# Linear attention and a two-layer MLP on one core: q of the first 512 tokens in runs of four, shared output banks, and a written order up to layer 1

## The chip, the core and the metric

The kernel runs on one core of one Trainium2 chip. Its time is the device time of one execution in microseconds, the median of the runs. A core has TensorE (PE; weight loads are listed as PEld), VectorE (DVE), ScalarE (ACT), GpSimd (POOL) and SyncE (SP), each with a queue that runs in order, and 16 DMA engines that all queues share. SP issues the loads of q, k and v; POOL issues the weights, which are cast from float32 to bfloat16 on the way, and most of the output.

## What is computed

Causal linear attention with a decay per head, in blocks with a running state, for 4 sequences of 768 tokens, 8 heads of 64; then a two-layer MLP (512 to 2048 to 512) on the 3072 tokens. `lam` lies between 0.97 and 0.99.

```python
for b in range(nb):
    qb, kb, vb = q[:, :, sl], k[:, :, sl], v[:, :, sl]
    intra = np.einsum('bhic,bhjc->bhij', qb, kb) * Dmask        # lam**(i-j) for i >= j
    intra = np.einsum('bhij,bhjd->bhid', intra, vb)
    inter = np.einsum('bhid,bhde->bhie', qb * lam_pow, kv_state)
    out[:, :, sl] = intra + inter
    kv_state = lam_block * kv_state + np.einsum('bhsd,bhse->bhde', kb * rev_pow, vb)
x = out.transpose(0, 2, 1, 3).reshape(B * S, H * D)
h = x @ w_in
g = np.where(h >= 1, h, np.where(h <= -1, 0.0, (h + 1) ** 2 / 4))
return g @ w_out
```

## The kernel before

**The first 512 tokens.** They are worked in four units: unit u = 2*sc + r has the 256 tokens of half sc (0 or 1) and the four heads of group r. For each unit SP loads q, k and v (`e_load`, 256 KB each). Partition p holds tokens 2p and 2p+1 of the half for four heads, so each run in memory is two tokens of one head, 512 B. `e_cast` multiplies q and k by a table of powers of `lam` and writes bfloat16 (k on DVE, q on POOL), and casts v. `e_t` transposes q or k on TensorE (four 128 by 128 transposes), `e_tc` copies the result to SBUF. `e_upd` adds k times v to the running state in PSUM, `e_st` copies the state to SBUF. `e_s` forms the scores into two PSUM banks of the pool `pp_s` (one for each parity of the head), `e_m` multiplies them by the causal mask on DVE. `e_sp` multiplies the state by q and starts the output in two fresh banks of `pp_y`; `e_o` adds the masked scores times v. `e_x` copies the output as bfloat16 into `xT`, the input of layer 1, whose first 512 columns therefore hold even tokens ahead of odd ones within each 128.

**Then.** The rest of the tokens comes in chunks of 128 (`f_load`, `cast`, and so on, from chunk 4). Layer 1 (`f_l1`, 8 matmuls of 256 columns a group for the first 512 tokens) goes to a bank of `pp_h` or `pp_y`; `f_r` on ACT and `f_g` on DVE apply the activation; `f_l2` is layer 2; `f_y` copies, `f_out` writes. For the first 512 tokens `f_out` issues two DMAs for each 128 rows, one for even and one for odd tokens. The weights come in nine slices (`f_w`, `WSL`): two of `w_in` of 256 columns, three of 512, four of `w_out`. Slice 0 is issued once k of unit 2 has landed (`GATE_W`); the first load of chunk 4 waits for slice 7 (`GL`).

**What sets the order.** Nearly every step is an entry made by `add(key, engine, ns, function, needs, due=...)`. `run_plan` simulates the engines with these costs, picks on each engine the ready entry with the earliest due time, and emits the steps in that order; matmuls on zeros (`warm`) fill TensorE's gaps before layer 1. Two waits outside the plan matter: `e_o` of units 0 and 1 waits for a state copy, and that of units 2 and 3 drains TensorE first. The needs of the plan that the change touches:

```python
add(("s", "e", u), "PE", 250, lambda u=u: e_s(u),
    [("kT", "e", u), ("qT", "e", u), ("m", "e", u - 1, 1)], ...)
add(("sp", "e", u), "PE", 300, lambda u=u: e_sp(u),
    [("st", "e", u, 1), ("st", "e", u, 0), ("x", "e", u - 1, 0), ("x", "e", u - 1, 1), ("qT", "e", u)], ...)
```

So the scores of a unit wait for both masks of the unit before, and the output of a unit waits until the one before has been copied out.

Of the kernel before, what the change touches and what calls it, by code (L numbers as in the profile page):

```python
# [8 lines left out]
F32 = mybir.dt.float32  # L9
BF16 = mybir.dt.bfloat16  # L10
# [13 lines left out]
def kernel(  # L24
# [73 lines left out]
    pos_ei = const.tile([128, 2, 2], I32)  # L98
    nc.gpsimd.iota(pos_ei, pattern=[[2 * C, 2], [1, 2]], base=-S // 2, channel_multiplier=2)
# [4 lines left out]
    pos_e = const.tile([128, NE], F32)  # L104
# [28 lines left out]
    def tables(pos, n, name):  # L133
        arg = const.tile([128, n, H], F32, name="arg" + name)
        nc.vector.tensor_tensor(arg, _bc(pos, 2, H), _bc(ln_lam, 1, n), op=AX.mult)
        tk = const.tile([128, n, H], F32, name="tk" + name)
        nc.scalar.activation(out=tk, in_=arg, func=AF.Exp, scale=-1.0)
        tq = const.tile([128, n, H], F32, name="tq" + name)
        nc.scalar.activation(out=tq, in_=arg, func=AF.Exp)
        return tq, tk  # L140

    tab_e = tables(pos_e, NE, "e")
    mask2 = const.tile([128, 2, 2, 64], F32)
    mask2b = const.tile([128, 2, 2, 64], F32)
    for t, base in ((mask2, 0), (mask2b, 128)):
        nc.gpsimd.memset(t, 1.0)
        nc.gpsimd.affine_select(
            out=t, in_=t, compare_op=AX.is_ge, fill=0.0,
            base=base, pattern=[[-1, 2], [1, 2], [2, 64]], channel_multiplier=-2)
# [11 lines left out]
    tab = tables(pos, NCB, "d")  # L161
# [21 lines left out]
    ops, OPS = [], {}  # L183
# [12 lines left out]
    def run_plan(free):  # L196

        users = {x.key: [] for x in ops}
        for x in ops:
            x.needs = [OPS[y] for y in x.keys if y in OPS]  # L200
            for y in x.needs:
                users[y.key].append(x)
# [100 lines left out]
    def get_xT(s):  # L303
        if s not in xT:
            xT[s] = xp.tile([128, KO, MS], BF16, name="xT", tag="xT")
        return xT[s]
# [6 lines left out]
    def e_load(u, x):  # L313
        sc, r = divmod(u, 2)
        t = ld.tile([128, HR, 2 * D], F32, name=f"x{x}f", tag=f"x{x}f")
        s0 = sc * 2 * C
        ld_dma["e", u, x] = nc.sync.dma_start(  # L317
            out=t, in_=(q, k, v)[x][0, HR * r:HR * r + HR, s0:s0 + 2 * C, :].rearrange("h (p j) d -> p h (j d)", j=2))
        qkv_ld["e", u, x] = t

    def e_cast(u, x, eng):
        sc, r = divmod(u, 2)
        nm, dct = (("qs", qs), ("ks", ks), ("vs", vs))[x]
        t = qkp.tile([128, 2, HR, D], BF16, name=nm, tag=nm)
        dct["e", u] = t
        src = qkv_ld["e", u, x].rearrange("p h (j d) -> p j h d", j=2)
        if x == 2:
            (nc.scalar.copy if eng is nc.scalar else eng.tensor_copy)(t, src)
        else:
            eng.tensor_tensor(t, src, _bc(tab_e[x][:, 2 * sc:2 * sc + 2, HR * r:HR * r + HR], 3, D), op=AX.mult)  # L330
# [3 lines left out]
    def e_t(u, i):  # L334
        if i:
            pt = pp_o.tile([128, 2, 2, 2, 128], BF16, name="po", tag="po")[:, 0]
        else:
            if not qbank:
                qbank.append(pp_h.tile([128, 2, 2, 2, 128], BF16, name="ph", tag="ph"))
            pt = qbank[0][:, 0]  # L340
        ptt["e", u, i] = pt
        for j in range(2):
            for hp in range(2):
                nc.tensor.transpose(out=pt[:, j, hp, :],
                                    in_=(qs, ks)[i]["e", u][:, j, 2 * hp:2 * hp + 2, :].rearrange("p a d -> p (a d)"),
                                    identity=ident)
# [6 lines left out]
    def new_pu():  # L353
        pu[0] = pp_u.tile([128, 2 * HP, D], F32, name="pu", tag="pu")[:, 0:HP]

# [25 lines left out]
    def e_s(u):  # L381
        for par in range(2):
            pst["e", u, par] = pp_s.tile([128, 2, 2, 2, 64], F32, name="ps", tag="ps")
        for j in range(2):
            for hp in range(2):
                for par in range(2):
                    for a in range(2):
                        nc.tensor.matmul(pst["e", u, par][HD[a], j, hp, :, :],  # L388
                                         lhsT=kT["e", u][HD[par], j, hp, HD[a]],
                                         rhs=qT["e", u][HD[par], :, hp, HD[a]],  # L390
                                         start=True, stop=True, skip_group_check=True)

    def e_m(u, par):
        if par == 0:
            sc_sb["e", u] = scp.tile([128, 2, 2, 2, 128], BF16, name="sc", tag="sc")
        nc.vector.tensor_tensor(sc_sb["e", u][:, par], pst["e", u, par].rearrange("p j h a q -> p j h (a q)"),  # L396
                                _bc(mask2.rearrange("p j a q -> p j (a q)"), 2, 2), op=AX.mult)

    def e_sp(u):
        sc = u // 2  # L400
        po = pot["e", u] = [pp_y.tile([128, MS], F32, name="py", tag="py")[:, 0:256].rearrange("p (h q) -> p h q", h=2)
                            for _ in range(2)]
        for a in range(2):
            if sc == 0 and a == 0:
                continue
            for hp in range(2):
                for par in range(2):
                    nc.tensor.matmul(po[a][HD[par], hp, :].rearrange("p (j q) -> p j q", j=2),
                                     lhsT=ubt["e", u, a][HD[par], hp, :],
                                     rhs=qT["e", u][HD[par], :, hp, HD[a]],  # L410
                                     start=(hp == 0), stop=False, skip_group_check=True)
        e_upd(u, 1)

    def e_o(u):
        sc, po, after = u // 2, pot["e", u], u < NU - 2
# [15 lines left out]
    def e_x(u, a, eng):  # L431
        sc, r = divmod(u, 2)
        off = 2 * C * sc + C * a
        (nc.scalar.copy if eng is nc.scalar else eng.tensor_copy)(
            get_xT(0)[:, 2 * r:2 * r + 2, off:off + C], pot["e", u][a])
# [179 lines left out]
    def f_l1(s, ni, n, part, on_y):  # L615
# [3 lines left out]
        for j in range(n):  # L619
            for ko in range(KO):  # L620
                nc.tensor.matmul(ph[:, j * m:(j + 1) * m],  # L621
                                 lhsT=w_in_sb[:, ko, (ni + j) * 128:(ni + j + 1) * 128],
                                 rhs=xT[s][:, ko, part * m:(part + 1) * m],
# [57 lines left out]
    def f_out(s, ms):  # L681
        m0 = s * MS + ms * 128
        if s == 0:

            for j in range(2):
                nc.gpsimd.dma_start(out=out[m0:m0 + 128, :].rearrange("(p j) n -> j p n", j=2)[j], in_=osb[s, ms][HD[j], :])
        elif s < NST - 1:
# [10 lines left out]
    def l1_list(s):  # L698
        n = PARTS.get(s, 1)
        if s == 0:  # L700
            return [(1, s, i, p) for w, p in W0 for i in (4 * w, 4 * w + 2)]
# [29 lines left out]
    AFTER_W = {2: ("cast", "e", 3, 0), 3: ("cast", "e", 3, 2)}  # L731
# [10 lines left out]

    pos_, last_ld = 0, None
    for u in range(NU):
        for x in (0, 1, 2):
            add(("ld", "e", u, x), "SP", 590, lambda u=u, x=x: e_load(u, x), [last_ld], due=pos_ * 1e-3, dma=880, ring=0.5)
            pos_, last_ld = pos_ + 1, ("ld", "e", u, x)
# [7 lines left out]
    for i in range(len(WSL)):  # L755
        add(("w", i), "POOL", 900, lambda i=i: f_w(i), [AFTER_W.get(i), ("w", i - 1) if i else None, ("ld",) + GATE_W[i] if i in GATE_W else None],
            due=i * 1e-3, dma=2650 if WSL[i][2] - WSL[i][1] == 4 else 1800)

    for u in range(NU):
        sc, r = divmod(u, 2)  # L760
        od = T0 + (-7000, -5500, -3500, -2000)[u]
        for x, e in ((1, "DVE"), (0, "POOL"), (2, "ACT" if u == 2 else "POOL")):
            add(("cast", "e", u, x), e, 540 if x == 2 else {"DVE": 605, "POOL": 960}[e],
                lambda u=u, x=x, e=e: e_cast(u, x, eng_of(e)), [("ld", "e", u, x), ("cast", "e", u - 1, x)], extra=90)
        for i in (1, 0):
            add(("t", "e", u, i), "PE", mm(*[128] * 4), lambda u=u, i=i: e_t(u, i),
                [("cast", "e", u, i), (("qT", "kT")[i], "e", u - 1)], extra=FILL)
        e = "DVE" if u else "ACT"
        add(("kT", "e", u), e, 335 if e == "DVE" else 485, lambda u=u, e=e: e_tc(u, 1, eng_of(e)), [("t", "e", u, 1)], extra=95)
        add(("qT", "e", u), "ACT", 485, lambda u=u: e_tc(u, 0, nc.scalar), [("t", "e", u, 0)], extra=100)  # L770
# [4 lines left out]
            [("kT", "e", u), ("qT", "e", u), ("m", "e", u - 1, 1)], extra=FILL, mode=T64)  # L775
        add(("st", "e", u, 1), "ACT", 170, lambda u=u: e_st(u, 1, nc.scalar), [("up", "e", u)], extra=100)
        for par in range(2):
# [3 lines left out]
            [("st", "e", u, 1), ("st", "e", u, 0), ("x", "e", u - 1, 0), ("x", "e", u - 1, 1), ("qT", "e", u)], extra=FILL, mode=T64)  # L781
        add(("o", "e", u), "PE", 250 + 240 * (u >= NU - 2), lambda u=u: e_o(u),
            [("m", "e", u, 0), ("m", "e", u, 1), ("sp", "e", u), ("st", "e", u + 2, 0) if u < NU - 2 else None], due=od, extra=FILL, mode=T64)
        add(("st", "e", u + 2, 0), "ACT", 170, lambda u=u: e_st(u + 2, 0, nc.scalar), [("sp", "e", u)], extra=100)
        for a in range(2):
            e = "DVE" if u == NU - 1 and a else "ACT"
            add(("x", "e", u, a), e, 270, lambda u=u, a=a, e=e: e_x(u, a, eng_of(e)), [("o", "e", u)], extra=110)
# [63 lines left out]
    for n1, (_, s, i, p) in enumerate(l1_order):  # L851
# [4 lines left out]
        else:  # L856
            kx = [("x", s * CPS + (p + 1) * CPS // n - 1)]
        j = (i // n) % RW
        grp = n1 // RW
        add(("l1", n1), "PE", mm(*[MS // n] * (KO * n)), lambda a=(s, i, n, p, on_y[n1]): f_l1(*a),  # L860
            kx + [w_of(0, i + n - 1), prev[-2] if len(prev) > 1 else None, ("l1", n1 - 1)]
            + [("x", "e", NU - 1, 0), ("x", "e", NU - 1, 1)] * on_y[n1] + [("qT", "e", NU - 1), ("o", "e", NU - 1)] * (n1 == 1), due=l_due[1, s, i, p], extra=FILL)
# [9 lines left out]
    for n2, (_, s, ms, kg) in enumerate(l2_order):  # L872
# [20 lines left out]
        if kg == 3:  # L893
            add(("y", y), "ACT", 490, lambda a=(s, ms): f_y(*a), [("l2", n2), ("y", y - 1), ("st", y - OB)], extra=95)
            add(("st", y), "POOL" if s < NST - 1 else "SP", 1600 if s == 0 else 800 if s < NST - 1 else 550, lambda a=(s, ms): f_out(*a),
# [34 lines left out]
```

## Time and profile before

| | us |
|---|---|
| median of 3 runs | 207.84 (207.6 to 209.36) |
| the profiled execution | 207.5 |
| its span, first to last instruction | 205.8 |
| TensorE busy (matmul) | 196.9 (96% of the span) |
| DVE, ACT, POOL busy | 140.8, 120.4, 72.3 |
| chain that ended last | TensorE 91%, SP's issue 3%, DMA 3%, issue 2% |

The page's slices of 5.1 us show TensorE at 7 and 8 tenths in the first two and at 9 and above from the fourth to the one before the last, at a granted clock of 9 or more tenths throughout. The DMA engines are at 9 tenths up to about 150 us and at 4 or less after that. 27.26 MB are read and 6.29 MB written.

How to read the views: busy times are shares of an engine's own timeline; a matmul's record covers its way through the array, so matmuls that follow each other overlap. The chain of work that ended last is followed back from the last instruction, at each step to what released it. In a group's row, "idle before" is the time the engine waited just before these instructions and what ended the wait. Unit numbers are not in the rows; they follow from the order of the instructions.

### The profile page before, as it was taken

Reading aid. Unit: us, or ns where it says so; the run is one execution under the profiler, and the core shown is the slowest. Engines: PE = TensorE matmul, PEld = TensorE weight load, DVE = VectorE, ACT = ScalarE, POOL = GpSimd, SP = SyncE. Lnnn points to the kernel's source line nnn. Section 1 sums busy time; section 2 is a strip of 40 time slices with the busy share of each in tenths; the row PEclk is TensorE's granted clock in tenths of the full one; section 3 lists DMA queues with packets and bytes.
Section 4 is the critical chain, followed back from the end, with each engine's and each line's share of the span. In section 5 each row is a group of like instructions: output and inputs, shape, how many; then the busy total and the mean of one; then the engine's idle time right before and its main releaser. Section 6 shows DMA issues by size and latency. Waiting matters only on the chain.

```text
span 205.8 us, 6360 instructions
## 1 busy us (share of the span) xinstructions
PE 196.9 (96%) x2721; PEld 135.7 (66%) x2753; DVE 140.8 (68%) x251; ACT 120.4 (59%) x225; POOL 72.3 (35%) x95
## 2 busy tenths in 40 slices
PE   7789999999999999999999999999999999999994
PEld 2558875457867867767757777766766766666643
DVE  4694997254885985859985998978876656364510
ACT  4476763327676756675674877486585465463421
POOL 6898000264225363474365255445331011010000
PEclk9999999999999999999999999999999999999999
DMA  5999999999999999999999999999942011011112
GB/s 163 301 235 196 198 206 212 219 220 183 132 183 247 138 201 208 258 195 243 193 183 292 173 218 253 194 180 275 204 109 74 3 43 62 0 51 54 51 51 102
DMA packets 94909, 34.48 MB, mean 168 GB/s; under 512 B 82210, under 2 KB 93218, under 8 KB 94882
## 3 DMA queue, kind: packets, MB, share of 16 engines
q1 hardware_dynamic: 88464, 24.65, 70.5%
q0 software_dynamic: 6416, 9.44, 20.6%
q8 instruction: 21, 0.34, 0.7%
q14 instruction: 6, 0.05, 0.1%
q10 hardware_dynamic: 2, 0.00, 0.0%
HBM read 27.26 MB, written 6.29 MB: 163 GB/s over the span
## 4 chain that ended last, share of the span: by engine, by line
PE 91%; SPq 3%; DMA 3%; issue 2%; DVE 0%; ACT 0%
PE ph L621 41%; PE py L654 38%; SPq L317 3%; DMA x1f<-in_k_dram 3%; PE py L664 2%; PE ps L515 1%; PE py L621 1%; PE ps L507 1%; PE pu L542 1%; PE po L542 1%; PE po L526 1%; PE py L423 1%; PE pu L526 0%; DVE ks L330 0%; PE ps L571 0%
## 5 line engine op out<-in xcount | busy, mean ns | idle before, releaser
L621 PE MATMUL ph<-xT,w_in_sb 128*128 128x256 bf16 (+1 forms) x872 | 94.0, 257 | 0.0
L629 ACT ACTIVATE r<-ph,one 128x512 bf16<-128x512 f32 x93 | 63.8, 687 | 45.2 <-PE ph L621 38.7
L621 PEld LDWEIGHTS <-w_in_sb 128*128 128x128 bf16 x896 | 76.3, 98 | 19.6 <-issue 0.2
L654 PE MATMUL py<-w_out_sb,gT 128*128 128x512 bf16 x338 | 86.0, 379 | 2.3 <-issue 1.1
L654 PEld LDWEIGHTS <-gT 128*128 128x128 bf16 x368 | 34.9, 98 | 28.4
L637 DVE TENSOR_SCALAR t<-r 128x1024 bf16<-128x1024 bf16 x48 | 22.5, 468 | 32.8 <-ACT r L629 32.4
L645 DVE TENSOR_TENSOR gT<-w,t 128x1024 bf16<-128x1024 bf16 x48 | 39.0, 812 | 1.4
L640 DVE TENSOR_TENSOR w<-r,t 128x1024 bf16<-128x1024 bf16 x48 | 38.8, 808 | 1.6
L468 POOL TENSOR_TENSOR kq<-x1f,tkd 128x512 bf16<-128x512 f32 x18 | 20.4, 1131 | 33.2 <-DMA x1f<-in_k_dram 23.4
L468 POOL TENSOR_TENSOR kq<-x0f,tqd 128x512 bf16<-128x512 f32 x18 | 19.7, 1093 | 23.8 <-DMA x0f<-in_q_dram 23.7
L688 POOL DMA_DIRECT2D out_dram<-osb x16 | 9.2, 573 | 32.6 <-ACT osb L679 32.6
L679 ACT COPY osb<-py 128x512 f32<-128x512 f32 x23 | 13.5, 585 | 11.3 <-PE py L654 6.9
L580 DVE TENSOR_TENSOR sd<-ps,diag 128x256 bf16<-128x256 f32 x36 | 13.5, 417 | 3.7 <-PE ps L515 3.5
L458 ACT CAST vs<-x2f 128x512 bf16<-128x512 f32 x20 | 12.4, 618 | 4.9 <-DMA x2f<-in_v_dram 4.5
L554 DVE TENSOR_TENSOR st<-st,ps 128x256 f32<-128x256 f32 x30 | 12.5, 415 | 0.5
L559 ACT CAST us<-st 128x512 bf16<-128x512 f32 (+1 forms) x18 | 10.4, 579 | 1.3 <-DVE st L554 1.2
L465 POOL TENSOR_TENSOR kq<-x0f,tqd 128x512 bf16<-128x512 f32 x2 | 2.4, 1178 | 20.8 <-DMA x0f<-in_q_dram 20.8
L563 ACT CAST xT<-po 128x256 bf16<-128x256 f32 x18 | 6.8, 377 | 4.5 <-PE pu L526 4.0
L563 ACT CAST xT<-pu 128x256 bf16<-128x256 f32 x18 | 6.7, 374 | 2.3 <-PE po L526 2.3
L542 PEld LDWEIGHTS <-vs 64*64 64x64 bf16 x288 | 3.7, 107 | 6.5 <-issue 5.9
L396 DVE TENSOR_TENSOR sc<-ps,mask 128x512 bf16<-128x512 f32 x8 | 5.2, 682 | 2.1 <-PE ps L388 2.1
L515 PE MATMUL ps<-vs,kq 64*64 64x64 bf16 x264 | 6.2, 196 | 0.0
(96 smaller groups left out, 134.3 us busy)
## 6 DMA issues: line engine op xcount, KB each, us to landing
x0f<-in_q_dram SPq DMA_DIRECT2D x24, 256.0 KB, 5.6
x1f<-in_k_dram SPq DMA_DIRECT2D x24, 256.0 KB, 4.8
x2f<-in_v_dram SPq DMA_DIRECT2D x24, 256.0 KB, 5.4
out_dram<-osb POOLq DMA_DIRECT2D x16, 256.0 KB, 4.0
w_out_sb<-in_moe_w_out_dram POOLq DMA_DIRECT2D x4, 512.0 KB, 14.4
w_in_sb<-in_moe_w_in_dram POOLq DMA_DIRECT2D x3, 512.0 KB, 7.8
out_dram<-osb POOLq DMA_DIRECT2D x8, 128.0 KB, 4.6
out_dram<-osb SPq DMA_DIRECT2D x3, 256.0 KB, 2.0
```

The costliest lines, as they stand in the source:

```text
L458: (nc.scalar.copy if eng is nc.scalar else eng.tensor_copy)(t, qkv_ld[c, x])
L468: eng.tensor_tensor(t.rearrange("p (i g) d -> p g i d", g=2), qkv_ld[c, x].rearrange(h4, g=2), tb.rearrange(h4, g=2), op=AX.mult)
L554: nc.vector.tensor_tensor(st[c][:, a], st[c][:, 0] if a else st[c - 1][:, 1], kv[c][a], op=AX.add)
L563: nc.scalar.copy(out=get_xT(s)[:, :, off:off + 64], in_=po_of(c, a))
L580: nc.vector.tensor_tensor(sc_sb[c][:, par], pst[c, par], _bc(diag, 1, HP), op=AX.mult)
L621: nc.tensor.matmul(ph[:, j * m:(j + 1) * m], lhsT=w_in_sb[:, ko, (ni + j) * 128:(ni + j + 1) * 128], rhs=xT[s][:, ko, part * m:(part + 1) ...
L629: nc.scalar.activation(out=r_t[grp][:, i, :], in_=ph_t[s, ni, part], func=AF.Relu, bias=one[:, 0:1])
L637: nc.vector.tensor_scalar(t_t[grp], r, 0.5, 1.0, op0=AX.mult, op1=AX.min)
L640: nc.vector.tensor_tensor(w_t[grp], r, t_t[grp], op=AX.subtract)
L645: nc.vector.tensor_tensor(gT[s][:, f - RW * n:f, part * m:(part + 1) * m], w_t[grp].rearrange("p a (b m) -> p (a b) m", m=m), t_t[grp].rea ...
L654: nc.tensor.matmul(py_t[s, ms], lhsT=gT[s][:, ko, ms * 128:(ms + 1) * 128], rhs=w_out_sb[:, ko, :], start=(ko == 0), stop=(ko == FO - 1))
L679: nc.scalar.copy(out=osb[s, ms], in_=py_t[s, ms])
```

## The change

- **q in runs of four.** Partition p of the first 512 tokens' q holds tokens 4p to 4p+3. A q load now covers two heads and all 512 tokens (256 KB, runs of 1 KB); q load u has heads 2u and 2u+1. A block of 128 tokens is 32 partitions, so a unit's q operand is four runs of 32 columns out of two of the transposed tiles. k and v stay in runs of two. The scores of units 0 and 2 (and 1 and 3) thus need q loads 0 and 1 (2 and 3). The table has one part for q and one for k, the mask's columns follow, and the exponentials for q come before those for k.
- **xT in token order.** `e_x` writes with a step of four elements, layer 1 of the first 512 tokens reads two runs of 128 columns, and `f_out` issues one DMA for 128 rows instead of two.
- **Banks.** Units 0 and 1 (and 2 and 3) share the two output banks, half each; `e_sp` of an odd unit waits for `e_o` of the unit before and no longer for its copies. The scores of unit 3 go to a bank of `pp_h` and the one of `pp_o`, and no longer wait for the masks of unit 2. Only unit 3 drains TensorE before its output.
- **Order.** The loads go q0 k0 q1 v0 q2 q3 k1 v1 k2 v2 k3 v3 instead of q, k, v of each unit. For TensorE, ACT, DVE and POOL a written list (`ORD`) chains each entry to the one before it, and says which engine takes which step; the planner orders only what comes after. In it, the letter is the step, the digits the unit and the operand or half (c: cast, t: transpose, 0 for q, 1 for k, 2 for v; w: weight slice; l1 and a digit: group of layer 1).
- What moves between engines: q casts 0, 1, 2 from POOL to DVE; v cast 2 from ACT to POOL; copies kT0 and qT1 to DVE, kT2 and kT3 to ACT; x copies 1 (first half) and 3 (first half) to DVE, 3 (second half) to ACT.

```diff
-        for j in range(2):
-            nc.gpsimd.dma_start(out=out[m0:m0 + 128, :].rearrange("(p j) n -> j p n", j=2)[j], in_=osb[s, ms][HD[j], :])
...
+        if x == 0:
+            t = ld.tile([128, 2, NE * D], F32, name="x0f", tag="x0f")
+            src = q[0, 2 * u:2 * u + 2, 0:MS, :].rearrange("h (p j) d -> p h (j d)", j=NE)
...
+    def e_q(u, hp, a):
+        b = 32 * (2 * (u // 2) + a)
+        return qT["e", 2 * (u % 2) + hp].rearrange("p a b q -> p (a b) q")[:, :, b:b + 32]
...
-            pst["e", u, par] = pp_s.tile([128, 2, 2, 2, 64], F32, name="ps", tag="ps")
+            pl, nm = ((pp_s, "ps"), (pp_s, "ps"), (pp_h, "ph"), (pp_o, "po"))[par + 2 * (u == NU - 1)]
+            pst["e", u, par] = pl.tile([128, 2, 2, 128], F32, name=nm, tag=nm)
...
+        if u % 2 == 0:
+            pyu[:] = [pp_y.tile([128, 2, 2, 128], F32, name="py", tag="py") for _ in range(2)]
+        po = pot["e", u] = [t[:, u % 2] for t in pyu]
...
-        sc, po, after = u // 2, pot["e", u], u < NU - 2
+        sc, po, after = u // 2, pot["e", u], u not in DRAINS
...
-            get_xT(0)[:, 2 * r:2 * r + 2, off:off + C], pot["e", u][a])
+            get_xT(0)[:, 2 * sc + a, 2 * r:2 * r + 2, :].rearrange("p h (q j) -> p h j q", j=NE),
+            pot["e", u][a].rearrange("p h (j q) -> p h j q", j=NE))
...
-    AFTER_W = {2: ("cast", "e", 3, 0), 3: ("cast", "e", 3, 2)}
+    DRAINS = (3,)
...
+    EL = [(int(y[1]), "qkv".index(y[0])) for y in "q0 k0 q1 v0 q2 q3 k1 v1 k2 v2 k3 v3".split()]
+    ORD = {
+        "PE": "t00 t01 t10 up0 s0 t20 sp0 t30 t11 o0 up1 s1 sp1 t21 up2 o1 s2 t31 sp2 s3 up3 o2 l10 sp3 o3 l11 l12",
+        "ACT": "qT0 st01 qT2 st20 qT3 st11 x01 x00 st30 kT2 st21 x11 kT3 st40 st31 x20 x21 r0 st50 x31 r1",
+        "DVE": "c00 c01 c10 kT0 qT1 c20 m00 c11 m01 kT1 c21 m10 m11 c31 x10 m20 m21 m30 m31 x30",
+        "POOL": "c02 c30 c12 w0 c22 w1 c32 w2 w3",
+    }
...
+    for l in ORD.values():
+        for y, z in zip(l, l[1:]):
+            CHAIN[z] = y
```

## The prediction

> **What bounds the kernel now.** I read the table of stretches first. Its columns are the stretch in us, then busy time (and number of instructions) of PE, PEld, DVE, ACT and POOL, the granted clock, the DMA share and GB/s.
> ```profile
> core 0: us, PE busy (x) PEld busy (x) DVE busy (x) ACT busy (x) POOL busy (x), PEclk, DMA share, GB/s
> ...
> 5.00:10.00 5.00, 3.65 (x72) 2.52 (x74) 3.22 (x5) 2.13 (x6) 4.01 (x5) 1.00 1.19 302
> 10.00:14.00 4.00, 3.25 (x102) 2.25 (x96) 3.41 (x7) 2.98 (x10) 4.00 (x5) 1.00 1.25 260
> 14.00:16.00 2.00, 1.77 (x60) 1.36 (x60) 1.59 (x4) 1.11 (x3) 2.00 (x4) 1.00 1.38 172
> ...
> 18.20:30.00 11.80, 11.75 (x106) 10.08 (x105) 10.10 (x18) 8.62 (x13) 1.51 (x4) 1.00 1.23 202
> ...
> 120.00:140.00 20.00, 19.82 (x253) 13.80 (x255) 17.78 (x31) 14.20 (x28) 10.31 (x11) 1.00 1.20 213
> ```
> From 18.2 us on, TensorE is busy 99% of the time. The table of waits from there to 195 us names no wait of TensorE but 1.1 us of "issue". The end is therefore the moment at which dense work begins plus a fixed amount of it. Only the 18 us before can give or take time, unless the change opens a new hole later.
>
> Next the chain that ended last, for those 18 us (start, duration, what):
> ```profile
> 7.75 5.38 DMA x1f<-in_k_dram
> ...
> 13.16 0.92 DVE ks L330
> ...
> 14.12 0.40 PE po L344 x4
> ...
> 15.09 0.64 PE py L423 x16
> 15.73 0.34 PE ps L388 x16
> ...
> 16.19 1.04 PE ph L621 x8
> ...
> 17.80 0.42 PE py L423 x16
> 18.21 0.98 PE ph L621 x8
> ```
> The eleventh of twelve loads (k of unit 3) lands at 13.13, DVE scales it, and TensorE then has no gap. So the load stream starts this path. From 5 to 10 us it moves 302 GB/s; the landings of v0, q1, k1, v1, q2, k2 (5.96, 6.80, 7.75, 8.61, 9.53, 10.42) stand 0.9 us apart.
>
> A second path ends at the same place. The first weight slice is issued by POOL at 10.71, and its issue row says how long it takes:
> ```profile
> w_in_sb<-in_moe_w_in_dram POOLq DMA_DIRECT2D x1, 256.0 KB, 5.4
> ```
> It lands at 16.11; the first layer-1 group starts at 16.19. Its issue waits for k of unit 2 (10.42).
>
> Last the groups by shape, for the price of each step (busy us, mean ns, idle before):
> ```profile
> L396 DVE TENSOR_TENSOR sc<-ps,mask 128x512 bf16<-128x512 f32 x8 | 5.2, 682 | 2.1 <-PE ps L388 2.1
> ...
> L330 POOL TENSOR_TENSOR qs<-x0f,tqe 128x512 bf16<-128x512 f32 x4 | 4.2, 1050 | 0.6 <-ACT tqe L139 0.5
> ...
> L330 DVE TENSOR_TENSOR ks<-x1f,tke 128x512 bf16<-128x512 f32 x4 | 3.6, 907 | 1.1 <-DMA x1f<-in_k_dram 1.1
> ...
> L351 ACT COPY qT<-ph 128x512 bf16<-128x512 bf16 x4 | 2.3, 585 | 1.9 <-PE ph L344 1.8
> ...
> L423 PE MATMUL py<-sc,vs 64*64 64x128 bf16 x64 | 2.1, 221 | 0.6 <-DVE sc L396 0.3 <-ACT ue L379 0.2
> ...
> L388 PE MATMUL ps<-qT,kT 64*64 64x128 bf16 x64 | 1.7, 222 | 0.3 <-ACT kT L351 0.3
> ...
> L351 DVE COPY kT<-po 128x512 bf16<-128x512 bf16 x3 | 1.2, 410 | 0.0
> ```
>
> **Loads.** Four q loads change from 512 B to 1 KB runs, and all four move to the first six places. k of unit 3 stays eleventh, now with four q loads before it, as before. A 512 B packet of the first 20 us holds an engine 31 ns (61.3% of 16 engines over 6336 packets); the 2 KB output packets hold it 86 ns. On the line between them 1 KB costs 49 ns against 62 for two halves, so 0.9 us becomes 0.71. The bounds are 0.6 (the step from 256 B at 26 ns to 512 B at 31 ns, carried on) and 0.9 (no gain). I take 0.75, nearer the row of the same direction and size class than a gain of a third. Four times 0.15 is 0.6, less a little since the first is mostly start-up: k of unit 3 at 12.6 instead of 13.13.
>
> [...]
>
> **The first weight.** Its gate, k of unit 2, moves from eighth to ninth: 10.42 + 0.9 - 0.5 = 10.8. On POOL it also stands behind three casts; the last, v of unit 1 (eighth load, 9.9), takes 0.84 at most 1.07, so POOL is free at 10.8 to 11.0. Issue at 10.85, 0.15 later. With the same 5.4 us it lands at 16.25; if the loads being over 0.4 us sooner frees engines for it, at 15.8. The later slices stand behind v of units 2 and 3 on POOL (about 12.5 and 14.3 against 11.57 and 13.42), but slice 1 had its first packet only when slice 0's were through (14.5 us in the packet records), so they are still queued ahead of need. Slice 2 has 0.9 us in hand at its first use (landed 20.0, used 20.94).
>
> **DVE.** It takes three q casts from POOL, swaps transposed copies with ACT (kT0 and qT1 in, kT2 and kT3 out) and takes one x copy of unit 1. Up to the cast of k3 its list holds six casts, three copies, four masks: 6 x 0.68 + 3 x 0.41 + 4 x 0.65 = 7.9 us. 0.68 is the smallest of its casts (0.68 to 1.20); the long ones ran beside POOL's q multiply, of which one is left. It starts when the q table is ready, 4.65, so 12.6 without waits; waiting for k1 and for that POOL multiply adds 0.1 to 0.5. I take 13.0 as start of the cast, against 13.16, and 13.7 as its end, against 14.07. The half microsecond won on the loads is thus not passed on: DVE's own queue is next.
>
> [...]
>
> **TensorE to the first layer-1 group.** After 13.7: transpose 0.40 (behind the scores of unit 2), copy of kT3 on ACT 0.59 instead of DVE 0.41 but before the masks of unit 2 rather than behind them: 14.8. The scores of unit 3 now have banks of their own and don't wait for the masks of unit 2: 14.85 to 15.2; state update to 15.4. Masks of unit 2 on DVE: 13.7 + 0.42 (x of unit 1) + 2 x 0.65 = 15.4, so its output runs 15.45 to 15.87, 0.42 without the drain against 0.64 with it. The first layer-1 group can start at 15.9, 0.3 earlier than 16.19, but the weight comes between 15.8 and 16.25, so I put it at 16.1. The rest to 18.21 (2.02 us: group, state outputs, output of unit 3 with its drain) is unchanged; unit 3's masks end at 16.7 and wait for nothing. Dense work starts 0.1 us earlier.
>
> **Costed at nothing.** Shared output banks lift a wait of TensorE on x that was on no path. Operands in four runs of 32, and layer 1's in two of 128: scores with two runs of 64 take 222 ns and outputs with one run of 128 take 221; if shorter runs did cost 10 ns each time, layer 1's 128 matmuls would lose 1.3. The wider table (32 more elements) and one more 0.13 us iota lie before 4 us, under the wait for lam. The stride in x's write is bounded by the 0.38 us row and hidden by the next group. Four output DMAs fewer save POOL 4 x 0.55 us around 45 to 60 us, where it is idle over half. After layer 1 the planner moves one second-layer group ahead of the transposes of chunk 4; its x, ready at 46.27 against a use at 47.90, moves 0.86 later and keeps 0.75.
>
> **Sum.** Profiled run 207.5 (span 205.8, 1.7 around it), minus 0.1. Against the median 207.84: 207.7.
>
> **Rivals.** A measurement of this kernel can tell about 1% (2.1 us) from no change.
> 1. *Both paths close sooner* (chance 0.2): DVE never waits and the weight lands at 15.8. Cast of k3 at 12.7, first group at 15.8: 0.4 off, 207.4. For it: DMA is emptier. Against: DVE's sum leaves no slack. A gain over 2 us would need the group before 14.1, half a microsecond after the cast of k3 ends: 0.03.
> 2. *The forecast*, within 0.3 of 207.7: 0.47.
> 3. *The weight comes late* (0.22), on the other side: if 1 KB runs gain nothing, k of unit 2 lands at 11.32, the weight is issued at 11.35 and lands at 16.75; the first group starts 0.6 late: 208.4. It decides as soon as the weight lands after 16.2. For it: TensorE had 0.08 us in hand. Against: the packet times.
> 4. *One in-order list holds up the others* (0.08): four hand-written lists must mesh, and any instruction that waits holds all behind it, as v3's cast holds slice 2 on POOL. If slices 2 to 8 come 3 us late, each first use waits and 2 us are lost: 209.8; or the clock falls in a startup with other gaps, and 8 us at half rate cost over 2. The clock row says 1.00 throughout.
>
> That the change does not do what it says, in the case that the masks of unit 2 still hold the scores of unit 3, would be +0.3, inside the range.
>
> The range 206.9 to 208.8 reaches over cases 1 to 3, with 0.5 below the first and 0.4 above the third for what the bounds of the loads and the spread of the runs (207.6 to 209.36) add; case 4 and the large gain, 0.11 together, are left out. Faster by over 1%: 0.03; within: 0.47 + 0.20 + 0.22 = 0.89; slower: 0.08.
>
> **What would show it.** k3 landing near 12.6 and k2 near 10.8; the cast of k3 starting when DVE's last mask of unit 1 ends, not at the landing; POOL issuing the first slice at 10.9; the first layer-1 group at 16.1; no new TensorE wait after 18 us. A wait of TensorE on w_in, or rows after 18 us slower than 0.87 us a group, would make it wrong.

## The result, and the profile after

| | before | after |
|---|---|---|
| median of 8 runs each, us | 208.26 (207.6 to 209.36) | 210.09 (209.68 to 210.85) |
| the profiled execution, us | 207.5 | 209.9 |
| its span, us | 205.8 | 208.2 |
| k of unit 2 / k of unit 3 landed | 10.4 / 13.1 | 11.4 / 13.1 |
| cast of k of unit 3 on DVE | 13.16 to 14.07 | 13.48 to 14.16 |
| slice 0 of w_in: issued / landed | 10.71 / 16.1 | 11.65 / 16.0 |
| slice 2 of w_in: issued / landed | 13.42 / 20.0 | 14.58 / 23.0 |
| layer-1 groups 1, 2, 5 start | 16.18, 18.14, 20.78 | 17.59, 19.93, 23.09 |

The changed kernel is slower by the ratio 1.0087, 95% interval 1.0058 to 1.0116: 1.8 us of 208. All of it is there by the fifth group of layer 1 (2.3 us later; the whole span is 2.4 longer). Of that, 1.79 is there at the second group, and 0.5 comes at the fifth.

The same stretches as before, of the kernel after:

```profile
core 0: us, PE busy (x) PEld busy (x) DVE busy (x) ACT busy (x) POOL busy (x), PEclk, DMA share, GB/s
...
10.00:14.00 4.00, 3.29 (x70) 2.54 (x70) 3.76 (x7) 2.33 (x5) 2.93 (x5) 0.57 0.98 222
14.00:16.00 2.00, 2.00 (x53) 1.49 (x55) 1.30 (x3) 1.62 (x4) 2.00 (x3) 0.50 1.05 131
16.00:18.20 2.20, 2.20 (x62) 1.96 (x57) 1.72 (x4) 1.44 (x5) 2.20 (x4) 0.69 1.12 156
18.20:30.00 11.80, 11.18 (x123) 9.30 (x122) 8.61 (x16) 8.95 (x15) 2.04 (x5) 1.00 1.19 190
```

Two columns differ. The granted clock is 0.57, 0.50 and 0.69 where it was 1.00, and TensorE is then busy all the time (2.00 of 2.00 us, was 1.77). And the DMA engines move 222, 131 and 156 GB/s where they moved 260, 172 and 203; the row of the kernel before for 16.0 to 18.2 us is this:

```profile
16.00:18.20 2.20, 2.09 (x57) 1.52 (x48) 1.29 (x2) 1.40 (x5) 2.20 (x4) 1.00 1.24 203
```

The chain that ended last goes through the DMA engines:

```profile
1.32 3.80 DMA x1f<-in_k_dram
5.12 0.02 issue
5.14 6.22 DMA x1f<-in_k_dram
11.36 0.30 issue
11.65 0.94 POOL w_in_sb L175
12.59 0.00 issue
12.59 0.62 POOL vs L337
13.22 0.69 POOL w_in_sb L175
13.91 0.03 issue
13.94 0.64 POOL vs L337
14.58 8.46 DMA w_in_sb<-in_moe_w_in_dram
23.04 0.04 issue
23.09 1.05 PE ph L637 x8
```

Read it upwards: the fifth group waits for slice 2, which was issued at 14.58 because POOL alternates slices and v casts from 11.65 on, and all of it stands behind k of unit 2. The chain no longer passes through a cast of DVE or through TensorE's unit 3. That does not make them innocent: a chain shows the path that came last, not the one that came second by 0.3 us, as the list of waits has it:

```profile
PE py L424 <- ACT xT L449: 0.7, 2, 0.6
...
PE ph L637 <- DMA w_in_sb<-in_moe_w_in_dram: 0.3, 1, 0.3
```

Had the slice been on time, the fifth group would have started 0.3 to 0.5 sooner, still 1.8 late. What the DMA engines did from 12 to 20 us, in 40 slices of 0.2 us (busy tenths and GB/s), first before, then after:

```profile
DMA  9999999999999999999999999999999999999999
GB/s 297 289 292 246 192 300 205 177 159 146 164 156 177 166 187 197 195 195 151 131 205 182 218 202 207 228 174 230 189 215 179 220 164 179 179 189 169 215 184 225
```

```profile
DMA  9976364699999994487999999877999789799999
GB/s 269 223 195 177 108 149 49 56 123 184 187 197 195 166 131 49 46 77 105 154 174 187 197 164 159 115 125 120 164 154 154 118 133 138 128 154 164 154 154 149
```

Before, slices 0 and 1 were issued back to back (10.71 and 11.66) and the queue never ran dry. After, they are issued at 11.65, 13.14 and 14.58, and the engines fall to 49 GB/s at 13.3 and to 46 at 15.2. The first of these dips lies between the end of the loads (13.4) and the first data of slice 0, the second between slices 0 and 1. In the packet records slices 0, 1 and 2 move their first packet 1.65, 2.0 and 2.0 us after their issue begins.

Last the copies of x to the input of layer 1 (before, then after; the 769 holds one of 0.85 us):

```profile
L434 ACT CAST xT<-py 128x256 bf16<-128x256 f32 x7 | 2.3, 375 | 1.0 <-PE py L423 0.9
...
L434 DVE CAST xT<-py 128x256 bf16<-128x256 f32 x1 | 0.4, 424 | 0.9 <-PE py L423 0.9
```

```profile
L449 ACT CAST xT<-py 128x256 bf16<-128x256 f32 x6 | 4.1, 769 | 0.4 <-PE py L439 0.3
```

```profile
L449 DVE CAST xT<-py 128x256 bf16<-128x256 f32 x2 | 1.5, 732 | 2.3 <-PE py L439 2.3
```

With bfloat16 written in a step of four elements the copy takes 0.73 us for 0.375 on ACT and 0.73 for 0.424 on DVE. That is also what the 0.6 us wait above is: the state outputs of unit 1 go into the bank that ACT still reads unit 0's output from (12.79, 0.56 us idle).

So there were three suspects: the order of the weights on POOL, the clock, and the copies of x.

### The profile page after: what moved, and what is told of

The parts are those of the page before. It is cut to its first block, busy times and chain, and to the rows that moved or that the text cites. A ratio compares the mean times of both kernels' runs of the same rounds, so it can differ in the third digit from the quotient of the medians.

```text
span 208.2 us, 6391 instructions
## 1 busy us (share of the span) xinstructions
PE 201.8 (97%) x2753; PEld 137.8 (66%) x2753; DVE 152.1 (73%) x255; ACT 121.0 (58%) x223; POOL 68.4 (33%) x90
## 4 chain that ended last, share of the span: by engine, by line
PE 87%; DMA 9%; POOL 1%; ACT 1%; issue 0%; SPq 0%; ACTq 0%
PE py L670 39%; PE ph L637 38%; DMA x1f<-in_k_dram 5%; DMA w_in_sb<-in_moe_w_in_dram 4%; PE py L680 2%; PE ps L531 1%; PE ps L523 1%; PE po L558 1%; PE pu L558 1%; PE py L637 1%; POOL w_in_sb L175 1%; PE po L542 1%; ACT r L645 1%; POOL vs L337 1%; PE pu L542 0%
## 5 line engine op out<-in xcount | busy, mean ns | idle before, releaser
L670 PE MATMUL py<-w_out_sb,gT 128*128 128x512 bf16 x368 | 90.8, 379 | 0.0
L653 DVE TENSOR_SCALAR t<-r 128x1024 bf16<-128x1024 bf16 x48 | 26.5, 551 | 26.4 <-ACT r L645 26.2
L661 DVE TENSOR_TENSOR gT<-w,t 128x1024 bf16<-128x1024 bf16 x48 | 43.4, 904 | 1.4
L484 POOL TENSOR_TENSOR kq<-x0f,tqd 128x512 bf16<-128x512 f32 x18 | 20.7, 1150 | 18.5 <-DMA x0f<-in_q_dram 18.3
L700 POOL DMA_DIRECT2D out_dram<-osb x20 | 11.4, 570 | 46.2 <-ACT osb L695 43.3
L695 ACT COPY osb<-py 128x512 f32<-128x512 f32 x23 | 13.5, 587 | 13.2 <-PE py L670 12.8
L596 DVE TENSOR_TENSOR sd<-ps,diag 128x256 bf16<-128x256 f32 x36 | 13.5, 414 | 2.7 <-PE ps L531 2.7
L575 ACT CAST us<-st 128x512 bf16<-128x512 f32 (+1 forms) x18 | 10.4, 578 | 5.5 <-DVE st L570 5.5
L481 POOL TENSOR_TENSOR kq<-x0f,tqd 128x512 bf16<-128x512 f32 x2 | 2.1, 1040 | 23.1 <-DMA x0f<-in_q_dram 23.1
L116 PE MATMUL ph<-zz 128*128 128x512 bf16 (+1 forms) x14 | 5.1, 511 | 1.3 <-DVE zz L104 1.3
```

Of the source, the lines that this page charges most:

```text
L484: eng.tensor_tensor(t.rearrange("p (i g) d -> p g i d", g=2), qkv_ld[c, x].rearrange(h4, g=2), tb.rearrange(h4, g=2), op=AX.mult)
L596: nc.vector.tensor_tensor(sc_sb[c][:, par], pst[c, par], _bc(diag, 1, HP), op=AX.mult)
L653: nc.vector.tensor_scalar(t_t[grp], r, 0.5, 1.0, op0=AX.mult, op1=AX.min)
L661: nc.vector.tensor_tensor(gT[s][:, f - RW * n:f, part * m:(part + 1) * m], w_t[grp].rearrange("p a (b m) -> p (a b) m", m=m), t_t[grp].rea ...
L670: nc.tensor.matmul(py_t[s, ms], lhsT=gT[s][:, ko, ms * 128:(ms + 1) * 128], rhs=w_out_sb[:, ko, :], start=(ko == 0), stop=(ko == FO - 1))
L695: nc.scalar.copy(out=osb[s, ms], in_=py_t[s, ms])
```

## The experiments

Each ran beside the kernel before on the same chip; the first four on one chip (before: 208.36, 17 runs), the next four on another (208.05, 15 runs), the last four on that one again (208.20, 35 runs). Lines of the diffs are those of the kernel after, but where the text says otherwise. A ratio given here is not the quotient of the two medians, from which it differs by up to 0.002; differences between variants that are smaller than that mean little.

**Slice 0 gated one load earlier**

```diff
-    GATE_W = {0: ("e", 2, 1)}
+    GATE_W = {0: ("e", 1, 2)}
```

> The changed kernel with one edit: weight slice 0 waits for v of unit 1 (landed 10.46 in the profile of the changed kernel) instead of k of unit 2 (11.36). Theory A (the stream of weight slices is the bound: it starts late, and its third slice lands at 23.04, when layer 1 needs it at 22.6): slice 0 is issued at about 11.1 instead of 11.65, the stream shifts by 0.5, slice 2 lands at about 22.5, the time falls by 0.4 to 0.5 and the wait of TensorE on w_in goes. Rival B (the path of TensorE to layer 1 is the bound, the weights only happen to be near): no change, within 0.2.

210.43 (209.99 to 210.62), ratio 1.0104 [1.007, 1.0138]. Slice 0 was issued at 11.71 all the same: on POOL it stands behind the cast of v of unit 1, which waits for the same load. An inconclusive run, but for one thing: the clock was at half here too (0.50 from 10 to 18.2 us), and the first group started at 18.43.

**Slice 2 ahead of the cast of v of unit 3**

```diff
-        "POOL": "c02 c30 c12 w0 c22 w1 c32 w2 w3",
+        "POOL": "c02 c30 c12 w0 c22 w1 w2 c32 w3",
```

> The changed kernel with weight slice 2 issued ahead of the cast of v of unit 3 on POOL (13.9 instead of 14.58). Theory A1 (slice 2 is late because its issue stands behind that cast): it lands 0.7 earlier, TensorE no longer waits for it, the time falls by about 0.5. Rival A2 (the DMA engines are still at slice 1 until 17.2, so the issue of slice 2 at 14.58 plus 1.9 us is not what holds it): slice 2 lands where it did, no change within 0.2.

209.86 (209.4 to 210.45), ratio 1.0078 [1.0051, 1.0106]. Slice 2 lands at 22.1, no group waits for it, and the loss stays: groups 1, 2, 5 start at 17.68, 20.03, 22.69. The weights alone are not the cause.

**x written without a step** (the output's first 512 rows then come in another order)

```diff
-            get_xT(0)[:, 2 * sc + a, 2 * r:2 * r + 2, :].rearrange("p h (q j) -> p h j q", j=NE),
-            pot["e", u][a].rearrange("p h (j q) -> p h j q", j=NE))
+            get_xT(0)[:, 2 * sc + a, 2 * r:2 * r + 2, :], pot["e", u][a])
```

> The changed kernel with x written without the step of four, so its rows of the first 512 tokens come out in another order within each 128. Each x copy should fall from 0.66 to 0.73 us to 0.38 to 0.42. Theory A (two paths, weights last): the first layer-1 groups come 0.5 to 0.9 us earlier, but group 4 still waits for slice 2 at 23.0, so the time stays within 0.2 and the wait on w_in grows. Rival C (the stride is the cause): the time falls by 0.8 or more.

210.01 (208.92 to 211.2), ratio 1.0078 [1.0048, 1.0109]. The copies are back at 0.377 and 0.423 us, the clock is at half from 11.1 to 17.9, the second group starts at 19.71, and the fifth at 23.28, because slice 2 lands at 23.2. The copies alone are not the cause either.

**The step moved to the matmuls that read q** (scores and state outputs read columns 256 B apart, so that x leaves in token order; the mask's columns and the write of x, whose lines are left out here, follow)

```diff
-        return qT["e", 2 * (u % 2) + hp].rearrange("p a b q -> p (a b) q")[:, :, b:b + 32]
+        return qT["e", 2 * (u % 2) + hp].rearrange("p a b q -> p q (a b)")[:, b:b + 32, :]
...
```

> The changed kernel with scores and outputs formed in token order instead: q is read with a step (4 elements 256 B apart) by the score and state-output matmuls, the mask's columns follow, and x is written without a step; the output is the reference's. If a matmul's moving operand in such short steps costs nothing, this equals the run with x written plainly (same time within 0.2); if it costs 50 ns per 128 columns, the 11 groups of 4 to 16 matmuls before layer 1 lose up to 1 us and the first layer-1 group is no earlier than in the changed kernel.

210.11 (209.62 to 210.66), ratio 1.0087 [1.0053, 1.0122]. The transposes of k and the outputs take 220 and 221 ns in the profiled run, so its clock was at full rate, and the slices went out as far apart as in the kernel after (11.99, 13.49, 15.10). It only swaps one price for another, by groups (score matmuls, then state outputs; 222 ns before the change):

```profile
L401 PE MATMUL ps<-qT,kT 64*64 64x128 bf16 x16 | 1.1, 389 | 0.0
...
L424 PE MATMUL py<-qT,ue 64*64 64x128 bf16 x4 | 0.6, 388 | 0.0
```

**All three first slices early in the kernel after** (v of unit 2 is cast by ACT, as before the change)

```diff
-        "ACT": "qT0 st01 qT2 st20 qT3 st11 x01 x00 st30 kT2 st21 x11 kT3 st40 st31 x20 x21 r0 st50 x31 r1",
+        "ACT": "qT0 st01 qT2 st20 qT3 st11 x01 x00 st30 c22 kT2 st21 x11 kT3 st40 st31 x20 x21 r0 st50 x31 r1",
-        "POOL": "c02 c30 c12 w0 c22 w1 c32 w2 w3",
+        "POOL": "c02 c30 c12 w0 w1 w2 c32 w3",
```

> The changed kernel with weight slices 0, 1 and 2 issued back to back on POOL as before the change, and the cast of v of unit 2 back on ACT. Theory A (the issues of the slices stand apart behind v casts, the DMA engines run dry between them): slice 1's first packet follows slice 0's last without a hole, slice 2 lands by about 21.5 and no wait on w_in is left; the time falls by 0.4 to 0.8, down to what TensorE's path allows (group 4 of layer 1 at 22.6). Rival B (TensorE's path alone): within 0.2 of the changed kernel.

210.15 (209.43 to 210.56), ratio 1.0098 [1.0066, 1.0129]. Slice 2 lands at 21.5, TensorE waits for no weight, and the groups start at 18.2, 20.54 and 23.2. TensorE's own way to layer 1 alone keeps the whole loss. Slice 2 is issued at 13.50, as in the kernel before (13.42), and still lands 1.4 later than there: slice 0 went out 1.1 later than there (11.82), and from 12.8 to 13.8, ahead of its data, the engines moved 20 to 87 GB/s.

**The old kernel with the slices set apart**

```diff
-    AFTER_W = {2: ("cast", "e", 3, 0), 3: ("cast", "e", 3, 2)}
+    AFTER_W = {1: ("cast", "e", 2, 2), 2: ("cast", "e", 3, 2)}
```

> The kernel before with one part of the change done alone: on POOL slice 1 is issued after the cast of unit 2's v and the multiply of unit 3's q, slice 2 after the cast of unit 3's v (about 13.5 and 14.9 instead of 11.7 and 13.4). Theory A: slice 2 lands at 22 to 23 instead of 20.0, group 4 of layer 1 waits for it from 20.9 on, the time rises by 1.0 to 2.0. Rival B (the slices have slack): no change within 0.3.

209.59 (208.84 to 211.03), ratio 1.0086 [1.0051, 1.0121]. Its slices go out at 11.07, 13.65 and 15.02. The clock stays at 1.00, groups 1 and 2 start at 16.3 and 18.27 as in the kernel before, and the fifth at 22.15 instead of 20.78. One wait is new, and the engines show why (12 to 20 us):

```profile
PE ph L621 <- DMA w_in_sb<-in_moe_w_in_dram: 1.1, 1, 1.1
```

```profile
DMA  9999999999996311999999999668669999999999
GB/s 292 292 287 253 236 282 197 192 195 189 187 169 69 36 23 20 97 141 184 189 177 182 187 133 67 41 36 92 92 97 174 256 184 189 184 179 169 215 179 205
```

From 14.4 to 15.2 and from 16.8 to 17.4 they run nearly empty. So the order of the slices alone, with nothing else of the change, costs as much as the whole change within the intervals (the span of its profiled run, the fastest of five, is 207.1 us against 205.8). Both theories hold, one beside the other: two paths, each late by nearly the full loss.

**Zero matmuls in the gaps, to hold the clock** (seven are added; the expectations count eight)

```diff
             x.fn()
+            for n in FILLS.get(x.key, ()):
+                warm(n)
...
+    FILLS = {("t", "e", 2, 0): (2,), ("sp", "e", 0): (4,), ("t", "e", 3, 0): (2,), ("t", "e", 1, 1): (4,), ("s", "e", 1): (4, 4), ("sp", "e", 1): (2,)}
```

> The changed kernel with eight more matmuls on zeros in TensorE's gaps between 8.7 and 13 us. Theory D (TensorE's clock is halved from 10.5 to 17.2 because it idles more): the granted clock stays at 1.00, the matmuls of units 1 to 3 take 0.42 instead of 0.66 a group, the first layer-1 group starts about 1 us earlier than 17.6; but slice 2 still lands at 23.0, so the time falls by at most 0.2. If the time falls by 1 us or more, the clock alone is the cause and theory A is wrong. If the clock falls all the same, idle time is not what halves it.

209.88 (209.03 to 210.87), ratio 1.0096 [1.0062, 1.013]. The clock is at 1.00 in the profiled run and groups 1 and 2 start at 16.47 and 18.81, 1.1 sooner than after. Nothing is won, because the other path is now last: slice 2 lands at 22.9 and the fifth group waits 1.3 us for it.

**All three edits** (slices early, zero matmuls, and x written in runs, with the step on the side that is read from PSUM)

```diff
-            get_xT(0)[:, 2 * sc + a, 2 * r:2 * r + 2, :].rearrange("p h (q j) -> p h j q", j=NE),
-            pot["e", u][a].rearrange("p h (j q) -> p h j q", j=NE))
+            get_xT(0)[:, 2 * sc + a, 2 * r:2 * r + 2, :].rearrange("p h (q j) -> p h q j", j=NE),
+            pot["e", u][a].rearrange("p h (j q) -> p h q j", j=NE))
```

> The changed kernel with three edits: slices back to back (and unit 2's v cast on ACT), the fill matmuls, and x written without a step, with the step in its reading of PSUM instead. If the two paths together explain the loss, TensorE starts layer 1 at about 16.3 and no slice is waited for: 1.8 to 2.4 us less than the changed kernel, about equal to before. If the x copy still takes 0.73 us, the step costs the same on the reading side. If it is still over 1 us slower than before, something else is behind the loss.

209.12 (208.38 to 210.73), ratio 1.0069 [1.004, 1.0097]. The copies take 0.377 and 0.424 us: the step costs nothing on the PSUM side. The runs fall into two groups. Five with a mean clock of 0.999 or 1.0 took 208.38 to 209.25; four of the five with 0.984 to 0.992 took 210.26 to 210.73 (the fifth 208.78). The profiled one is in the second group (210.29): its second load of q landed at 7.4, 1.2 later than in the kernel after, TensorE stood idle for 1.6 us over it, and the clock was at half from 9.1 to 12.5. Late loads and the clock thus come together in it, and the sorting of the runs can't part them.

**Slices early and x in runs, no zero matmuls**; diffs as above.

> The kernel after, with slices 1 and 2 of w_in issued ahead of the casts of v of units 2 and 3 and with x written without a step (the step is on the side that is read from PSUM); no zero matmuls added. If the doubled x copies are the main part of what TensorE lost on its way to layer 1, the first group starts at 16.5 to 17.0 and the time is 208.6 to 209.2. If the halved clock is the main part, the clock row still shows about 0.5 from 10 to 17 us, the first group starts at 17.5 to 18, no group waits for w_in, and the time is 209.6 to 210.2.

209.39 (208.56 to 210.41), ratio 1.0038 [1.0013, 1.0063]. The profiled run again had its second load of q late (7.4) and the clock at half, from 8.75 to 15.6; its first group started at 18.25. Its second group waited 0.45 us for slice 1, against both expectations: behind the late loads the slices went out only from 12.63 on. Against the 210.15 with the slices early alone, the copies are worth some 0.8 us at the median; the spread of the runs is as large.

**Slices early and zero matmuls, x with its step**

> The kernel after, with the slices early and with eight more zero matmuls in the gaps before 13 us, but with x still written with a step of 8 bytes. If the clock is the main part: clock near 1.0 in all rows, first group at 16.3 to 16.7, no wait for w_in, and 208.4 to 209.0, as the runs of the version with all three edits that kept the clock. If the x copies weigh as much: first group at 17 or later and 209.3 or more.

209.65 (208.31 to 211.02), ratio 1.0053 [1.0023, 1.0083]. The profiled run took 208.31: clock 1.00, groups at 16.65, 18.96 and 21.62, no wait for a weight. Again the clock sorts the runs: six with 0.999 or 1.0, median 208.87; six below, median 210.1.

**All three, slice 0 gated on k of unit 1, and three more zero matmuls at 6 to 8 us**

```diff
-    GATE_W = {0: ("e", 2, 1)}
+    GATE_W = {0: ("e", 1, 1)}
-        "POOL": "c02 c30 c12 w0 c22 w1 c32 w2 w3",
+        "POOL": "c02 c30 w0 c12 w1 w2 c32 w3",
...
+    FILLS = {("t", "e", 0, 1): (4, 4), ("t", "e", 1, 0): (2,), ...
```

> All three edits (slices early, x written without a step, zero matmuls), slice 0 gated on k of unit 1 and issued ahead of the cast of v of unit 1, and three more zero matmuls at 6 to 8 us, where TensorE stood idle for 1.6 us in the run whose clock fell. If idle time of TensorE sets the clock, it holds in most runs. Slice 0 is issued near 10.3 and takes bandwidth from k of unit 3, which may land 0.5 later (13.5). If the early weight is free: 207.6 to 208.4. If the loads pay for it: first group at 16.7 or later and 208.6 to 209.4.

208.17 (207.63 to 209.95), ratio 0.9995 [0.9967, 1.0023]: the loss is gone, and nothing is won. All 12 runs have a mean clock of 0.998 or more, which by itself proves little, as the next experiment shows; but the matmuls of 128 columns in the profiled run take 220 to 225 ns from 6 us on, which is full rate. It has slice 0 issued at 10.21, k of unit 3 landing at 13.5, groups at 16.89, 18.85 and 21.48, and no wait for a weight. The engines stay full from 12 to 20 us:

```profile
DMA  9999999999999999999999999999999999999999
GB/s 276 264 246 225 225 215 218 210 182 149 207 138 151 141 154 172 184 159 164 169 146 161 166 179 169 195 184 195 164 174 154 148 128 148 133 169 179 210 189 215
```

**The old kernel without the zero matmuls of its planner**

```diff
-                    warm(n)
+                    n and None
```

> The kernel before, without the zero matmuls that its planner puts into TensorE's gaps before layer 1; nothing else changes. If a clock that falls in the startup costs about 1 us or more by itself, the clock row falls to 0.5 somewhere from 8 to 17 us, the first group starts 0.5 to 1.5 later than 16.2, and the time is 208.6 to 209.8. If the gaps don't set the clock, or a fallen clock costs nothing there, the time is 207.8 to 208.3.

208.93 (207.83 to 210.55), ratio 1.0017 [0.9987, 1.0047]. Neither expectation was right as written: the clock column says 1.00 throughout, and yet the first group starts at 17.32. The durations explain it (6 to 16 us; 222 ns in the kernel before):

```profile
L344 PE MATMUL po<-ident,ks 128*128 128x128 bf16 x16 | 2.5, 309 | 0.2 <-DVE ks L330 0.2
...
L388 PE MATMUL ps<-qT,kT 64*64 64x128 bf16 x48 | 2.1, 310 | 0.0
```

309 ns are the 299 to 311 ns of the kernel after at half clock. The trace has no record of the clock before 16.48, and the column shows 1.00 there all the same, as it does in the kernel before ahead of its first record (6.09): by its matmuls the old kernel without zero matmuls ran the stretch from 6 to 16 us at half rate. Of the 1.1 us by which its first group is late, the loads of that run explain most: k of unit 3 landed at 14.0, 0.9 later than in the kernel before. From the end of its cast (15.06) to the first group are 2.26 us, where the kernel before needs 2.11 at full rate. So the old order hides nearly all of a halved clock; the new one doesn't, with 3.43 us after and 2.39 where the clock held (14.08 to 16.47, the run with zero matmuls only).

The other runs of the kernel before say the same. Of the 67 that ran beside these variants, 33 have a mean clock of 0.983 to 0.992 (worked out: 3.41 us at half rate make 0.992 of a span of 206 us, 6.83 make 0.983). Their medians are 0.6, 0.1 and 0.1 us above those of the other runs of their batch. The mean does not say where in a run the clock fell, but in every trace here with a mean below 0.998 it was within the first 21 us. So the old kernel seems to lose the clock in about half of its runs and to pay little for it. By the trace above a mean of 1.00 does not prove that the clock held; the sorting of runs by it in the last experiments is as coarse as that.

## Why the prediction was wrong

207.7 was predicted, 206.9 to 208.8; the median is 210.09. The rival with a chance of 0.08 is the one that came: slices late, "or the clock falls in a startup with other gaps". Both halves of it happened, where the text took them for alternatives of small chance. Two steps failed, the later slices and TensorE's way to layer 1, and either would have been enough.

**The later slices.** The step: "so they are still queued ahead of need. Slice 2 has 0.9 us in hand". The times of POOL's steps were right in kind (slices 1 and 2 at 13.14 and 14.58), and the slack was nearer 0.7 (the fifth group started at 20.78, not 20.94). What failed is the inference: that a slice's first packet waits for the end of the slice before was read as proof that the queue is full, and it was full only because two slices had been issued back to back. With 1.5 us between the issues, and each needing 1.65 us or more to its first data, the engines ran dry between slices 0 and 1 and every later slice moved by the hole; another hole came ahead of slice 0, issued at 11.65 for the 10.85 of the prediction. Slice 2 landed 3.0 us later for an issue 1.16 later. The step alone costs 1.0086 in the old kernel.

**TensorE to layer 1.** The step put the first group at 16.1 with durations at full clock, for which "The clock row says 1.00 throughout" was the only support. That row was read of one run of the kernel before, which by the means above seems to lose the clock in about half of its runs (33 of 67); it says nothing about how near the edge that run stood, nor what the new order would pay. In the profiled runs where the clock fell, it was at half for 3.4 us (all three edits), for 6.8 (five runs; 6.83 after) or for about 10.2 (slice 0 gated one load earlier). These are stretches of 3.41 us: of the kernel before the one that follows its first record of the clock, of the kernel after the one ahead of the fall and the two at half rate (before, then after):

```profile
6.09:9.50 3.41, 2.19 (x53) 1.68 (x52) 1.79 (x4) 2.09 (x5) 2.62 (x3) 1.00 1.21 301
```

```profile
7.11:10.52 3.41, 2.36 (x52) 1.62 (x51) 3.04 (x6) 1.23 (x4) 1.66 (x3) 1.00 1.10 307
10.52:13.94 3.42, 2.86 (x62) 2.28 (x63) 3.18 (x6) 2.12 (x5) 2.83 (x5) 0.50 0.94 212
13.94:17.35 3.41, 3.41 (x95) 2.82 (x98) 2.23 (x5) 2.34 (x5) 3.41 (x5) 0.50 1.13 144
```

Before, the clock held through a stretch with TensorE busy for 2.19 of 3.41 us (64%) and behind it; after, it fell behind one with 69%. In the other profiled runs cut this way, stretches ahead of a fall have 40 to 63% (1.36 of 3.42 us with all three edits, 2.15 of 3.41 with slice 2 ahead of the cast), and stretches that the clock held through 62% and more (2.13 of 3.42 in the old kernel with the slices set apart). The shares overlap, so this row can't tell which side a kernel is on. After the fall the clock was still at half behind a stretch with 84% (2.86 of 3.42, the second row after) and, with the slices early and x in runs, behind one with 90% (3.08 of 3.42); it was back behind one with 100% (3.41, the third row).

The clock's part of the 1.79 us at the second group is 1.1 (18.81 with the zero matmuls against 19.93), for 6.83 us at half rate; that "8 us at half rate cost over 2" was the author's estimate, and no run shows it. The loads and DVE are not in it: the cast of k of unit 3 ends only 0.1 late (14.16 for 14.07).

About 0.4 is the step in the write of x. Between the first and the second group TensorE needs 2.31 to 2.35 us in the five profiled runs that write x with its step and have the clock back by the first group (2.34 after). It needs 1.96 or 1.97 in the five that write x without it and have the clock by then (1.96 before). In the first kind it waits for the copy of x once more there, 0.18 us.

The last 0.3 comes from a wait that the prediction put at nothing: "transpose 0.40 (behind the scores of unit 2)". In the kernel before, the transposes of k of unit 3 begin when its cast ends (14.12 for 14.07), and at half rate too (15.12 for 15.06). In the written order the state update of unit 2, the output of unit 1 and the scores of unit 2 stand ahead of them. With the clock held they begin 0.57 us after the cast's end (14.65 for 14.08), of which 0.2 is won back on the way to the first group (1.82 us from there, for 2.06 before). In the kernel after they begin 1.06 after it:

```profile
13.48 0.68 DVE L339 TENSOR_TENSOR ks<-x1f,tke 128x512 bf16<-128x512 f32 x1
...
15.22 0.61 PE L354 MATMUL po<-ident,ks 128*128 128x128 bf16 x4
```

So a half-rate clock lengthens a queue that stands on the path, where the old order had the transposes first. From the end of the cast to the first group TensorE needs 3.4 us instead of 2.1, and it is busy without a gap from 13.94 to 17.35 (the third row above). With the clock held the first group started at 16.47, for the 16.1 of the forecast.

**Loads.** Mis-sized: k of unit 3 landed at 13.1 for 12.6, and the last byte of the loads came at 13.39, for 13.41 before. The four runs of 1 KB gained nothing in sum. A 1 KB packet holds an engine 52.6 ns in the packet records, close to the 49 of the estimate, and the stream dips at 3.6 to 4.6 us, behind the first two loads, to 230 GB/s where the kernel before moves 293. This is the third rival's condition (k of unit 2 at 11.36 for its 11.32). Its price did not come in the way it said, since slice 0 landed at 16.0, before TensorE was ready. That this lies inside the forecast 15.8 to 16.25 is luck: issued 0.8 us later than forecast, the slice took 4.3 us for the 5.4 of the row.

**Costed at nothing.** "Shared output banks lift a wait of TensorE on x" was the wrong way round: they add one, 0.56 us for unit 1. "The stride in x's write is bounded by the 0.38 us row" was no bound: 0.73. The step holds TensorE up by the 0.4 us above. What it is worth in the whole time is not settled: 0.8 us at the median with the slices early and the clock left alone (210.15 to 209.39), and 0.5 with the zero matmuls too (209.65 to 209.12), both inside the spread of the runs. The runs of 32 columns (222 ns a score matmul in the last variant, as before), the wider table (its argument takes DVE 0.32 us for 0.28), and the stretch after layer 1 cost nothing that shows: after the fifth group no new wait of TensorE appears, though DVE is busy for 152.1 us instead of 140.8.

**DVE** did in kind as predicted: the cast of k of unit 3 starts behind the masks, not at the landing, though at 13.48 for the forecast 13.0.

What stays open: in the last variant three things changed at once (the gate, the order on POOL, three zero matmuls), so which of them took the last 0.95 us of it (209.12 to 208.17) wasn't parted. And the second load of q landed anywhere from 6.0 to 7.4 in the profiled runs of the changed kernel and its variants; why was not found. The runs of 1 KB are not needed for it: in the old kernel without zero matmuls the third load, v in runs of 512 B, landed 2.2 us after the second.

## What to carry to other kernels

A full transfer queue hid the distance between two issues here (10.71 and 11.66: no dip); with 1.5 us between them the engines ran nearly dry (down to 46 GB/s after). So, before a step is put between two issues, ask what keeps the engines fed until the second has its first data (1.65 to 2.0 us after the issue began). When two paths end within half a microsecond of each other, removing one shows nothing: undo each alone in the new kernel, and do each alone in the old one. And a clock at full rate in the startup was the state of one run here (33 of 67 runs of the kernel before have a mean of 0.983 to 0.992): ask what the order would cost at half rate, and read the rate from the duration of one known matmul (222 or 309 ns), not from the column alone.

## What was not expected of the hardware

- The second load of q, 256 KB in runs of 1 KB, landed 1.1 to 2.9 us after the load ahead of it (5.1 to 6.2 after; 4.4 to 7.4 with all three edits); the later ones follow each other by 0.7 to 1.2.
- Where the trace holds no record of the clock yet, its column shows 1.00 (up to 6.09 us in the kernel before, to 7.11 in the one after): in the old kernel without zero matmuls, 309 ns for a transpose of 128 columns against 222 gave the half rate away.
- A bfloat16 write to SBUF with a step of 8 bytes took 0.73 us for 128x256 on ACT and on DVE, against 0.375 (ACT) and 0.424 (DVE) without it; reading PSUM with a step of 128 bytes instead took 0.377 and 0.424.
- A moving operand read with 256 B between columns took 389 ns for 128 columns against 222.
